# Four constants in one tile, and the two sides of SBUF moved by 32 and 96 bytes

## The chip, the cores and the metric

The kernel runs on one core of one Trainium2 chip. The metric is the time of one execution in device microseconds. Three runs of the kernel before gave 917.54, 922.28 and 922.48 us; their median is 922.28 us.

## The reference

Attention with pooled keys and values feeds a gated MLP, and this feeds a second MLP. With 4 batches, 8 heads, 576 positions and a head size of 64, in float32:

```python
k_p = k.reshape(B, H, 72, 8, D).mean(axis=3)          # pool 8 positions into one
v_p = v.reshape(B, H, 72, 8, D).mean(axis=3)
attn = softmax(q @ k_p^T / sqrt(D));  x = attn @ v_p   # -> x[2304, 512]
xn = x / sqrt(mean(x*x) + 1e-6) * rms_g
y = (silu(xn @ w_gate) * (xn @ w_val)) @ w_out         # 512 -> 1536 -> 512
h = y @ w_in2;  out = silu(h) @ w_out2                 # 512 -> 2048 -> 512
```

## The kernel before, in words

The 2304 tokens are eight chunks of 288 columns (`CH`). Activations stand transposed: features on the 128 partitions, tokens along the free dimension.

Nearly every product of the three MLP stages is made three times, so that float32 accuracy comes out of the faster matmul type `float32r`: each operand is split into a high and a low part of that type, and the kernel adds high by high, high by low and low by high. `mm3` (lines 256 to 259) and `mm3_open` (line 773) issue these triples. One tile of shape `[P, 2, n]` holds the high part first and the low part behind it, `4 n` bytes later in the same partition. For each matmul TensorE loads 128 columns of the stationary operand (a weight load, engine PEld) and streams the moving operand past it.

There are four large shapes of these float32r matmuls, by the number of moving columns:

- 288 columns, 9 groups of 240: the first MLP on chunks 0 to 4. Moving `xT` and `hT`, stationary `w_gate`, `w_val`, `w_out`.
- 432 columns, 9 groups of 96: the first MLP on chunks 5 to 7, taken as two halves of 432. Moving `xw` and `hw`, stationary the same weights.
- 384 columns, 1008: the way up of the second MLP (a Strassen-like scheme of 7 products), moving `xP1` to `xP7` (shown as `xP`), stationary `in`.
- 256 columns, 1512: its way down, moving `out2` (shown as `out`), stationary `hc`.

Besides these, chunks 2 to 7 of the attention make 3 products each for 4 head pairs with moving `pT` and stationary `vbd`, and one with moving `pR` (line 495); the scores (line 405) take `qT` as the stationary and `kbd` as the moving operand.

The order of all work is written out by hand in four long strings of steps (`start`, `pair`, `last`, `second`); nothing is rearranged by a scheduler. Every DMA is issued by the SP queue.

Where a tile lies decides the byte at which its rows begin. A tile pool takes the left side of SBUF, growing upwards, or the right side, growing downwards, and each tile's size is rounded up to 32 bytes. The pool `const` comes first on the left: `ident` with 512 bytes, then `ones`, `mhalf`, `g_sb` and `mask` with 32 bytes each, and later `scrap` with 32 bytes. On the left stand `stage`, `p1`, `att`, `pw` and `p2x`; on the right `w0`, `w1` (the weights of the first MLP, and the `early` tiles that share their places during the start) and `p2` (`h`, `s2`, `out2`).

In the program as built, the tiles that matter begin at these bytes past a multiple of 128:

| tiles | side | before |
|---|---|---|
| `xT`, `hT`, `xw`, `hw`, `xP`, `in`, `hc`, `kbd`, `vbd`, `vr`, `sq` | left | 32 |
| `w_gate`, `w_val`, `w_out`, `out2`, `h`, `early` tiles | right | 96 |
| `qT`, `pT`, `pR`, `kv`, `vs` (they lie behind three `kp` tiles of 288 bytes) | left | 0 |
| `ident` | left | 0 |

The low part lies 1152, 1536 or 1024 bytes behind the high part in the shapes of 288, 384 and 256 columns, which are multiples of 128, so both parts begin at the same remainder. In the shape of 432 columns it lies 1728 bytes behind, which adds 64 to the remainder.

Of the kernel before, what the change touches and what calls it, by code (L numbers as in the profile page):

```python
# [9 lines left out]
F32 = mybir.dt.float32  # L10
# [12 lines left out]
def tile_pooled_attention_then_two_mlps(  # L23
# [25 lines left out]
    P = 128  # L49
    KT = DM // P  # L50
# [5 lines left out]
    NTT = CH // TT  # L56
# [15 lines left out]
    EXP_SCALE = 1.0 / (POOL * math.sqrt(D))  # L72

    const = ctx.enter_context(tc.tile_pool(name="const", bufs=1))
    w_ctx = [ExitStack(), ExitStack()]
    w_pools = [x.enter_context(tc.tile_pool(name=f"w{i}", bufs=1, side="right")) for i, x in enumerate(w_ctx)]
    stage = ctx.enter_context(tc.tile_pool(name="stage", bufs=1))
# [13 lines left out]


    ident = const.tile([P, P], F32, name="ident")
    ones = const.tile([P, 1], F32, name="ones")
    mhalf = const.tile([P, NTT], F32, name="mhalf")
    g_sb = const.tile([P, KT], F32, name="g_sb")
    mask = const.tile([P, 4], F32, name="mask")

    def setup():
        make_identity(nc, ident)  # L100
# [1254 lines left out]
```

## Time and profile before

| | |
|---|---|
| runs | 917.54, 922.28, 922.48 us |
| the profiled execution, its own time | 922.12 us |
| its span, first to last instruction | 920.3 us |
| PE busy | 901.8 us, 98% of the span |
| weight loads (PEld) busy | 875.4 us, 95% |
| DVE, ACT, POOL busy | 631.2, 542.5, 375.8 us |
| mean granted clock of TensorE | 0.981 |

The profiled execution took 1.8 us more than its span, and 0.2 us less than the median. In the page's slices PE is at nine tenths or more in 38 of 40; the first slice has 5 and the last has 8. Matmuls overlap in the trace: one of 288 columns is shown with some 0.3 us, and the next one starts 0.13 us after it. So a shape's cost is read from the distance of starts, not from the mean length of one. How the matmuls' starts follow each other is read in the timeline; where many of one line follow each other it shows them as one row, with their count and their length from the first start to the last end.

### The profile page before, as it was taken

Reading aid. Unit: us, or ns where it says so; the run is one execution under the profiler, and the core shown is the slowest. Engines: PE = TensorE matmul, PEld = TensorE weight load, DVE = VectorE, ACT = ScalarE, POOL = GpSimd, SP = SyncE. Lnnn points to the kernel's source line nnn. Section 1 sums busy time; section 2 is a strip of 40 time slices with the busy share of each in tenths; the row PEclk is TensorE's granted clock in tenths of the full one; section 3 lists DMA queues with packets and bytes.
Section 4 is the critical chain, followed back from the end, with each engine's and each line's share of the span. In section 5 each row is a group of like instructions: output and inputs, shape, how many; then the busy total and the mean of one; then the engine's idle time right before and its main releaser. Section 6 shows DMA issues by size and latency. Waiting matters only on the chain.

```text
span 920.3 us, 17356 instructions
## 1 busy us (share of the span) xinstructions
PE 901.8 (98%) x6122; PEld 875.4 (95%) x6122; DVE 631.2 (69%) x1254; ACT 542.5 (59%) x1453; POOL 375.8 (41%) x487
## 2 busy tenths in 40 slices
PE   5999999999999999999999999999999999999998
PEld 4689999999999999999999998999999999999998
DVE  6789988765554835443368779658986579766675
ACT  5688887364254714345444546677666677576653
POOL 6435443344215621200027746881038910388200
PEclk8589999999999999999999999999999999999999
DMA  8645642342215321244367885266862668614486
GB/s 281 204 140 174 218 134 64 120 152 78 62 41 134 116 66 40 84 137 144 131 230 258 291 280 182 89 206 206 269 213 63 213 187 264 233 49 161 125 263 208
DMA packets 85259, 149.79 MB, mean 163 GB/s; under 512 B 8627, under 2 KB 53812, under 8 KB 85172
## 3 DMA queue, kind: packets, MB, share of 16 engines
q1 hardware_dynamic: 85172, 148.68, 50.0%
q8 instruction: 48, 0.79, 0.4%
q14 instruction: 39, 0.32, 0.1%
HBM read 116.21 MB, written 32.44 MB: 162 GB/s over the span
## 4 chain that ended last, share of the span: by engine, by line
PE 81%; DVE 9%; DMA 4%; POOL 3%; issue 2%; ACT 1%; SPq 0%; ACTq 0%; POOLq 0%; DVEq 0%
PE P L773 38%; PE pv L257 4%; PE pv L259 4%; PE pv L258 4%; PE pg L258 4%; PE pg L257 4%; PE pg L259 4%; PE acc L258 4%; PE acc L257 4%; PE acc L259 4%; PE sc L405 2%; PE pT L456 1%; PE pv L491 1%; DMA out<-out2s 1%; DMA xw_raw<-xw 1%
## 5 line engine op out<-in xcount | busy, mean ns | idle before, releaser
L773 PE MATMUL P<-xP,in 128*128 128x384 f32 x1008 | 179.5, 338 | 0.7 <-POOL in L244 0.5
L773 PEld LDWEIGHTS P<-xP,in 128*128 128x128 f32 x1008 | 177.5, 188 | 1.6 <-POOL in L244 0.8
L773 PE MATMUL P<-out,hc 128*128 128x256 f32 x1512 | 172.7, 276 | 0.0
L773 PEld LDWEIGHTS P<-out,hc 128*128 128x128 f32 x1512 | 172.5, 188 | 0.0
L244 POOL TENSOR_TENSOR in<-in,in 128x256 fp32r<-128x256 f32 x96 | 78.8, 830 | 112.1 <-ACT in L237 64.5
L237 ACT ACTIVATE hc<-h 128x384 fp32r<-128x384 f32 x144 | 74.1, 525 | 41.8 <-PE P L773 37.7
L244 DVE TENSOR_TENSOR hc<-h,hc 128x384 fp32r<-128x384 f32 x144 | 81.6, 590 | 19.6 <-ACT hc L237 17.7
L257 PE MATMUL pg<-xT,w_gate 128*128 128x288 f32 x240 | 73.0, 304 | 0.8 <-DVE hT L244 0.8
L257 PE MATMUL pv<-xT,w_val 128*128 128x288 f32 x240 | 73.0, 304 | 0.1
L257 PE MATMUL acc<-hT,w_out 128*128 128x288 f32 x240 | 72.4, 302 | 0.0
L258 PE MATMUL pg<-xT,w_gate 128*128 128x288 f32 x240 | 71.6, 298 | 0.2
L258 PE MATMUL acc<-hT,w_out 128*128 128x288 f32 x240 | 71.2, 297 | 0.2 <-DVE hT L244 0.2
L259 PE MATMUL pg<-xT,w_gate 128*128 128x288 f32 x240 | 71.2, 297 | 0.0
L259 PE MATMUL pv<-xT,w_val 128*128 128x288 f32 x240 | 70.9, 295 | 0.0
L258 PE MATMUL pv<-xT,w_val 128*128 128x288 f32 x240 | 70.8, 295 | 0.0
L259 PE MATMUL acc<-hT,w_out 128*128 128x288 f32 x240 | 70.8, 295 | 0.0
L423 ACT ACTIVATE pr<-sc,mx 96x72 f32<-96x72 f32 x192 | 57.9, 314 | 17.8 <-DVE mx L416 17.8
L624 ACT ACTIVATE th<-pg 128x288 f32<-128x288 f32 x57 | 23.5, 413 | 72.1 <-PE pg L259 71.9
L244 POOL TENSOR_TENSOR in<-sums,in 128x256 fp32r<-128x256 f32 x72 | 59.0, 829 | 2.4 <-ACT in L237 2.0
L626 DVE SCALAR_TENSOR_TENSOR th<-th,pg 128x288 f32<-128x288 f32 x57 | 25.6, 448 | 40.1 <-ACT th L624 40.0
L257 PEld LDWEIGHTS pg<-xT,w_gate 128*128 128x128 f32 x240 | 45.7, 190 | 1.3 <-issue 1.0
L258 PEld LDWEIGHTS pg<-xT,w_gate 128*128 128x128 f32 x240 | 45.6, 190 | 0.6 <-DVE xT L244 0.6
(233 smaller groups left out, 2304.4 us busy)
## 6 DMA issues: line engine op xcount, KB each, us to landing
out<-out SPq DMA_DIRECT2D x84, 512.0 KB, 4.7
out<-out2s SPq DMA_DIRECT2D x56, 256.0 KB, 4.1
in<-in SPq DMA_DIRECT2D x24, 512.0 KB, 3.6
raw<-in_moe_w_out_dram SPq DMA_DIRECT2D x18, 512.0 KB, 4.5
raw<-in_moe_w_in_dram SPq DMA_DIRECT2D x16, 512.0 KB, 3.7
early_raw<-in_moe_w_gate_dram SPq DMA_DIRECT2D x10, 512.0 KB, 4.2
early_raw<-in_moe_w_val_dram SPq DMA_DIRECT2D x10, 512.0 KB, 4.9
early_raw<-in_moe_w_out_dram SPq DMA_DIRECT2D x10, 512.0 KB, 4.8
```

Of the source, the lines that this page charges most:

```text
L237: nc.scalar.activation(out=out, in_=in_, func=AF.Copy, scale=1.0 if scale is None else scale)
L244: ENGINES[engine[0] or usual].tensor_tensor(out=out, in0=in0, in1=in1, op=op)
L257: nc.tensor.matmul(ps, lhsT=whi, rhs=xhi, start=first, stop=False)
L258: nc.tensor.matmul(ps, lhsT=whi, rhs=xlo, start=False, stop=False)
L259: nc.tensor.matmul(ps, lhsT=wlo, rhs=xhi, start=False, stop=last)
L405: nc.tensor.matmul(ps[:TT, a * 2 * SP:(a + 1) * 2 * SP], lhsT=qT[:, a * TT:(a + 1) * TT], rhs=kbd[:, j, :], start=True, stop=True,)
L423: nc.scalar.activation(out=pr[:, a, e], in_=s4[:, a, e], func=AF.Exp, bias=mx[:, a, e:e + 1], accum_out=sm[:, a, e],)
L456: nc.tensor.transpose(ps[:n, a * TT:(a + 1) * TT], src, ident[:TT, :TT])
L491: nc.tensor.matmul(ps, lhsT=vr0[:RR, j, :], rhs=pT_t[c, NPAIR + j // 2], start=False, stop=True)
L624: nc.scalar.activation(out=th, in_=pg, func=AF.Tanh, scale=0.5)
L626: nc.vector.scalar_tensor_tensor(out=th, in0=th, scalar=1.0, in1=pg, op0=ALU.add, op1=ALU.mult)
L773: nc.tensor.matmul(ps, lhsT=a, rhs=b, start=first and n == 0, stop=n == 2, skip_group_check=True)
```

## The change

Two unused tiles are added, and the four constants become slices of one tile `small`:

```diff
     const = ctx.enter_context(tc.tile_pool(name="const", bufs=1))
+    edge = ctx.enter_context(tc.tile_pool(name="edge", bufs=1, side="right"))
+    edge.tile([P, 24], F32, name="edge")
...
     ident = const.tile([P, P], F32, name="ident")
-    ones = const.tile([P, 1], F32, name="ones")
-    mhalf = const.tile([P, NTT], F32, name="mhalf")
-    g_sb = const.tile([P, KT], F32, name="g_sb")
-    mask = const.tile([P, 4], F32, name="mask")
+    small = const.tile([P, 16], F32, name="small")
+    ones, mhalf, g_sb, mask = (small[:, a:b] for a, b in ((0, 1), (1, 1 + NTT), (4, 4 + KT), (8, 12)))
+    const.tile([P, 8], F32, name="align")
```

`edge` takes 96 bytes at the right end, so every tile of the right side begins 96 bytes lower. On the left 64 bytes (`small`) and 32 (`align`) stand where 128 stood, so every tile behind them begins 32 bytes lower. The bytes past a multiple of 128 become:

| tiles | before | now |
|---|---|---|
| `xT`, `hT`, `xw`, `hw`, `xP`, `in`, `hc`, `kbd`, `vbd`, `vr`, `sq` | 32 | 0 |
| `w_gate`, `w_val`, `w_out`, `out2`, `h`, `early` tiles | 96 | 0 |
| `qT`, `pT`, `pR`, `kv`, `vs` | 0 | 96 |
| `ident` | 0 | 0 |
| low part of `xw`, `hw` | 96 | 64 |

A tile of the right side stood 64 bytes off one of the left, counted in remainders of 128, and now stands at the same remainder; two tiles of the same side keep their distance. No instruction is added, removed or moved: each engine has the same instructions in the same order with the same waits as before, and only the name `small` and the addresses differ.

## Rows read from the trace of the kernel before

**Rows 1.** Page: span, part 1, the chain that ended last by engine

```profile
span 920.3 us, 17356 instructions
PE 901.8 (98%) x6122; PEld 875.4 (95%) x6122; DVE 631.2 (69%) x1254; ACT 542.5 (59%) x1453; POOL 375.8 (41%) x487
...
PE 81%; DVE 9%; DMA 4%; POOL 3%; issue 2%; ACT 1%; SPq 0%; ACTq 0%; POOLq 0%; DVEq 0%
```

**Rows 2.** Groups by shape, PE: line, tiles, shapes, count, busy us, mean ns, idle

```profile
L773 PE MATMUL P<-xP,in 128*128 128x384 f32 x1008 | 179.5, 338 | 0.7 <-POOL in L244 0.5 <-ACT in L237 0.2
L773 PE MATMUL P<-out,hc 128*128 128x256 f32 x1512 | 172.7, 276 | 0.0
L257 PE MATMUL pv<-xT,w_val 128*128 128x288 f32 x240 | 73.0, 304 | 0.1
...
L257 PE MATMUL pg<-xw,w_gate 128*128 128x432 f32 x96 | 34.6, 360 | 0.0
...
L257 PE MATMUL pv<-pT,vbd 128*128 128x288 f32 x24 | 7.4, 310 | 0.0
```

**Rows 3.** Waits of PE: line, released by, us in total, times, longest

```profile
PE sc L405 <- POOL kbd L241: 8.9, 3, 7.3
```

**Rows 4.** Timeline of PE, 288 columns: start us, us, instruction

```profile
99.79 0.30 PE L258 MATMUL pv<-xT,w_val 128*128 128x288 f32 x1
...
104.30 0.29 PE L259 MATMUL pg<-xT,w_gate 128*128 128x288 f32 x1
```

**Rows 5.** Timeline of PE, 432 columns

```profile
499.77 0.36 PE L257 MATMUL pg<-xw,w_gate 128*128 128x432 f32 x1
...
502.71 0.36 PE L257 MATMUL acc<-hw,w_out 128*128 128x432 f32 x1
```

**Rows 6.** Timeline of PE, 384 and 256 columns, runs of matmuls in one row

```profile
599.78 3.51 PE L773 MATMUL P<-xP,in 128*128 128x384 f32 x19
...
911.73 4.81 PE L773 MATMUL P<-out,hc 128*128 128x256 f32 x41
```

**Rows 7.** Timeline of PE, products of the attention among those of an expert

```profile
209.33 0.30 PE L257 MATMUL pv<-pT,vbd 128*128 128x288 f32 x1
...
209.73 0.29 PE L495 MATMUL pv<-pR,vr 96*128 96x288 f32 x1
209.86 0.29 PE L257 MATMUL acc<-hT,w_out 128*128 128x288 f32 x1
...
211.44 0.30 PE L257 MATMUL pv<-pT,vbd 128*128 128x288 f32 x1
```

**Rows 8.** Groups by shape, weight loads (PEld) from 60 to 916 us

```profile
L405 PEld LDWEIGHTS sc<-kbd,qT 128*96 128x96 f32 x132 | 16.9, 163 | 0.2 <-ACT kbd L237 0.2
...
L528 PEld LDWEIGHTS ms<-ones,sq 128*96 128x96 f32 x36 | 3.7, 164 | 0.3
```

**Rows 9.** Groups by shape, DVE

```profile
L244 DVE TENSOR_TENSOR pT<-pT 128x288 fp32r<-128x288 f32 x24 | 10.9, 455 | 5.5 <-ACT pT L237 5.1
...
L244 DVE TENSOR_TENSOR hT<-pv,hT 128x288 fp32r<-128x288 f32 x21 | 9.4, 449 | 0.4 <-ACT hT L237 0.2
...
L342 DVE TENSOR_REDUCE kp<-kv 128x72 f32<-128x576 f32 x9 | 6.6, 739 | 0.0
...
L342 DVE TENSOR_REDUCE kp<-early 128x72 f32<-128x576 f32 x5 | 3.7, 733 | 3.5 <-DMA early<-in_k_dram 3.5
```

**Rows 10.** The chain in order of time, its first transfer: start us, us, what

```profile
1.22 4.26 DMA early<-in_k_dram
```

**Rows 11.** DMA issues: KB each, median us to landing

```profile
out_dram<-o SPq DMA_DIRECT2D x12, 128.0 KB, 3.5
```

**Rows 12.** Stretches: length, busy us of PE, PEld, DVE, ACT, POOL; granted clock

```profile
20.00:51.00 31.00, 30.46 (x106) 20.74 (x105) 22.29 (x48) 21.69 (x90) 16.01 (x23) 0.50 0.50 159
...
200.00:300.00 100.00, 100.00 (x776) 99.96 (x774) 55.34 (x129) 45.19 (x158) 39.30 (x60) 1.00 0.30 90
```

## The prediction

> **What bounds the kernel now.** I read the page first: PE is busy for 901.8 of 920.3 us, and the chain that ended last lies on PE for 81% of the span [rows 1]. Then PE's waits, to see whether that busy time is a queue without holes: the largest is 8.9 us in 3 waits at the scores of the start, one of them 7.3 us before the first matmul [rows 3]. The idle 920.3 - 901.8 = 18.5 us is thus this 8.9, the tail after the last matmul, and crumbs. Third the groups by shape, for the counts [rows 2]: 9 groups of 240 matmuls with 288 columns (2160), 9 of 96 with 432 (864), 1008 with 384, 1512 with 256. The mean length in these rows includes the overlap with the next matmul, so the price of one is read from the distance of starts in the timeline:
>
> - 288 columns: 35 matmuls begin from 99.79 to 104.30 us, both ends counted, so 4.51 / 34 = 132.6 ns [rows 4];
> - 432: 16 from 499.77 to 502.71, so 2.94 / 15 = 196.0 ns [rows 5];
> - 384: a run of 19 lasts 3.51 us, less the 0.338 us of the last [rows 2] over 18 steps: 176.2 ns [rows 6];
> - 256: a run of 41 lasts 4.81 us, less 0.276 over 40 steps: 113.4 ns [rows 6].
>
> Times the counts: 286.4 + 169.3 + 177.6 + 171.5 = 804.8 us, 87% of the span. So only two things can move the time much: the distance of starts of these 5544 matmuls, or new holes between them. The change adds and moves no instruction and no wait, so what is left is whether an instruction takes another time when its operands begin at other bytes.
>
> **The change part by part.**
>
> *Matmuls, the moving operand.* The trace has this experiment inside it: `pT` and `pR` begin at a multiple of 128 bytes, `hT` at 32 past one. At 209.33 us three products with moving `pT` and one with `pR` stand amid those of an expert, all of 288 columns: four steps from 209.33 to 209.86, 0.53 / 4 = 132.5 ns, and the twelve steps with moving `hT` after them, from 209.86 to 211.44, take 1.58 / 12 = 131.7 ns [rows 7]. The aligned operand is no faster; with starts rounded to 0.01 us, 0.8 ns is about what the rounding allows. So the moving operand's start byte costs nothing while the stationary operand begins at 32 or 96. I take 0.
>
> [...]
>
> *Matmuls, the stationary operand.* In the large shapes it begins at 32 or 96 in the whole trace; the nearest rows are weight loads of float32 with 96 columns at full clock: from `qT`, at 0, they take 163 ns, from `sq`, at 32, 164 ns [rows 8]. That is again no difference, but on loads that are not limited by a stream at full rate, so it is weaker evidence. I take 0 here too, because the row is near and the other ends below have no row that shows them.
>
> *Both ends for these two.* [...] A nearer end is the best rate that the kernel shows: 113.4 / 256 = 0.443 ns a column. At that rate the others take 127.6, 191.4 and 170.1 ns: 5.0 x 2160 + 4.6 x 864 + 6.1 x 1008 ns = 10.8 + 4.0 + 6.1 = 20.9 us less. From above: the worst rate is that of 288 columns, 0.460; with it the shapes of 256, 384 and 432 would take 117.8, 176.6 and 198.7: 4.4 x 1512 + 0.4 x 1008 + 2.7 x 864 ns = 6.7 + 0.4 + 2.3 = 9.4 us more.
>
> *Tiles that lose their start.* `qT`, `pT`, `pR`, `kv` and `vs` go from 0 to 96. By the same rows [7, 8] this costs nothing. If a misplaced start did cost a matmul 6 ns, the 72 products with `pT` (three groups of 24 [rows 2]) would give 0.4 us: too little to count.
>
> *The other engines.* They matter in the first 60 us, where PE waits for them, and wherever a buffer is late. The same instruction on tiles at both starts: DVE subtracts into `pT` (at 0) in 455 ns and into `hT` (at 32) in 449; it reduces `kv` (at 0) in 739 ns and an `early` tile (at 96) in 733 [rows 9]. A per cent, and against the aligned tile. I take 0; at 1% of the chain's DVE share of 9% [rows 1] it would be 0.8 us either way.
>
> *DMA.* Only the first load (4.26 us, into an `early` tile [rows 10]) and the last store (3.5 us [rows 11]) lie on the path with nothing beside them. Were they a tenth quicker or slower, it would be 0.8 us. The rest lands while PE works off its queue.
>
> *The small tile.* Two memsets, one reduction and one load write other bytes of it than before, and each reader reads its own slice. The waits are those of before, so no writer waits for another's slice: 0.
>
> Sum: 922.12 us of the profiled execution, of which 920.3 are its span, plus 0: 922.1 us, against a median of 922.28. I say 922.
>
> **The rivals.**
>
> *A, faster: the start byte does cost, but only goes away when both operands are aligned.* [...] Against it: the aligned `pT` should then have shown a part, and showed none [rows 7]. [...] Price: if all shapes came to the best rate, 20.9 us, so 901.
>
> [...]
>
> *B, slower: equal remainders collide.* The weight load reads SBUF while the stream does. In the shapes of 256 and 288 columns one operand lies left and the other right, 64 bytes apart in the remainder; now they are equal. [...] It would decide if 256 columns rose from 113.4 to about 117.8 ns: the 9.4 us from above, 931. Against it: per column 384 (0.459) is no worse than 288 (0.460), whose operands are 64 apart, and 432, where the low part has the remainder of the weights and the high part has not, has 0.454, between the others.
>
> *C, the change does not do what it says for the operands that count.* The low parts of `xw` and `hw` come to 64, and `pT` and `qT` lose their alignment. Their shares are 864 / 3 = 288 matmuls and the small ones above; whichever way starts matter, this turns A or B by some 2 us and is inside their prices.
>
> **How the numbers follow.** No change 0.50: the rows with both starts agree on three engines. A 0.30: the combination that it needs is in no row, and it touches 87% of the span. B 0.20: the rows are nearly as much against it, and it touches less. What this measurement can tell from no change is about 0.5%, 4.6 us: the runs before lie 4.9 us apart. A at 901 is beyond it, and so is B at 931, so these are the chances of faster and slower. The range goes from A's price, 901, to just short of B's, 930; below it lies the part of A that goes towards 868 or 855, above it the part of B that is worse than its price, together under 2 in 10. The forecast's own range is 917 to 926.
>
> **What would show it.** Right: starts of 288, 432, 384 and 256 columns 132.6, 196.0, 176.2 and 113.4 ns apart within 1 ns, waits of PE as before. [...] B: 256 columns rises while 384, whose operands keep their distance, stays at 176. The forecast would be wrong if any one of the four distances moved by more than 2 ns, or if PE waited anew while they stay.

## The result, and the profile after

The changed kernel takes 930.39 us (median of 6 runs, 927.34 to 931.68) against 922.25 us (6 runs beside them, 917.54 to 923.48): ratio 1.0091, 95% interval 1.0071 to 1.0112. It is slower, by 0.9%, and 0.4 us above the top of the range that was given.

The page of the changed kernel, with the lines that answer to [rows 1]:

```profile
span 929.9 us, 17356 instructions
PE 910.1 (98%) x6122; PEld 883.9 (95%) x6122; DVE 632.2 (68%) x1254; ACT 541.8 (58%) x1453; POOL 376.3 (40%) x487
...
PE 79%; DVE 10%; DMA 5%; POOL 3%; issue 2%; ACT 2%; SPq 0%; ACTq 0%; POOLq 0%; DVEq 0%
```

The count of instructions is the same, and DVE, ACT and POOL are busy as long as before within 1.0 us. PE has 8.3 us more of busy time in a span that is 9.6 us longer. Its groups by shape, against [rows 2] (line numbers are one higher; columns as there):

```profile
L774 PE MATMUL P<-out,hc 128*128 128x256 f32 x1512 | 180.7, 282 | 0.0
L774 PE MATMUL P<-xP,in 128*128 128x384 f32 x1008 | 179.4, 338 | 0.7 <-POOL in L245 0.4 <-ACT in L238 0.3
L258 PE MATMUL pv<-xT,w_val 128*128 128x288 f32 x240 | 73.2, 305 | 0.0
...
L258 PE MATMUL pg<-xw,w_gate 128*128 128x432 f32 x96 | 34.5, 359 | 0.0
...
L258 PE MATMUL pv<-pT,vbd 128*128 128x288 f32 x24 | 7.5, 314 | 0.0
```

One row moved: 256 columns, from 172.7 to 180.7 us. 384 columns (179.5 to 179.4) did not. PE's waits, against [rows 3], are the same within 0.4 us but for 0.9 us at the start, which is a wait of the attention's first scores:

```profile
PE sc L406 <- POOL kbd L242: 9.8, 3, 7.0
```

The cleanest view of the price is a place where nearly a third of the 256-column matmuls follow each other as one row of the timeline, and then a third of those of 384. Start, length, instruction, count; before:

```profile
744.74 55.30 PE L773 MATMUL P<-out,hc 128*128 128x256 f32 x486
799.88 58.37 PE L773 MATMUL P<-xP,in 128*128 128x384 f32 x330
```

and after:

```profile
749.02 57.94 PE L774 MATMUL P<-out,hc 128*128 128x256 f32 x486
806.79 58.34 PE L774 MATMUL P<-xP,in 128*128 128x384 f32 x330
```

The row of 486 less the mean length of its last matmul, over 485 steps: (55.30 - 0.276) / 485 = 113.45 ns before, as in [rows 6], and (57.94 - 0.282) / 485 = 118.88 ns after. The step of 384 columns is 176.4 and 176.3 ns. So 5.43 x 1512 = 8.2 us lie in this one shape. Over all steps between two following matmuls of a shape at the full clock (1.00 granted from 60 us on), 288 columns went from 132.54 to 133.08 ns and 432 from 195.4 to 196.2: 0.54 x 2160 + 0.8 x 864 = 1.9 us more. Together 10.1 us, where the span shows 9.6. The longer wait at the start is not felt behind it: after 200 matmuls, at 59.5 us, the changed kernel is only 0.1 us behind.

### The profile page after: what moved, and what is told of

It reads as the page before. It is cut to its first block, busy times and chain, and to the rows that moved or that the text cites. A ratio compares the mean times of both kernels' runs of the same rounds, so it can differ in the third digit from the quotient of the medians.

```text
span 929.9 us, 17356 instructions
## 1 busy us (share of the span) xinstructions
PE 910.1 (98%) x6122; PEld 883.9 (95%) x6122; DVE 632.2 (68%) x1254; ACT 541.8 (58%) x1453; POOL 376.3 (40%) x487
## 4 chain that ended last, share of the span: by engine, by line
PE 79%; DVE 10%; DMA 5%; POOL 3%; issue 2%; ACT 2%; SPq 0%; ACTq 0%; POOLq 0%; DVEq 0%
PE P L774 38%; PE pv L258 4%; PE pv L260 4%; PE pv L259 4%; PE pg L259 4%; PE pg L258 4%; PE pg L260 4%; PE acc L259 3%; PE acc L258 3%; PE acc L260 3%; PE sc L406 2%; DMA out<-out2s 1%; PE pT L457 1%; DMA raw<-in_moe_w_out_dram 1%; PE pv L492 1%
## 5 line engine op out<-in xcount | busy, mean ns | idle before, releaser
L774 PE MATMUL P<-out,hc 128*128 128x256 f32 x1512 | 180.7, 282 | 0.0
L774 PEld LDWEIGHTS P<-out,hc 128*128 128x128 f32 x1512 | 180.5, 190 | 0.0
L774 PE MATMUL P<-xP,in 128*128 128x384 f32 x1008 | 179.4, 338 | 0.7 <-POOL in L245 0.4
```

Source lines behind the costliest of these rows:

```text
L774: nc.tensor.matmul(ps, lhsT=a, rhs=b, start=first and n == 0, stop=n == 2, skip_group_check=True)
```

## The experiments

In what follows the *distance* is the first byte of the moving operand less that of the stationary operand, as a remainder of 128. The recorded expectations speak of these theories. **D**: the distance decides (rival B of the prediction, put more widely). **S**: a start at 0 itself is bad for the streams. **N** and **O**: a stream collides with the load of the next block, or with that of its own. **H**: address bits above 128 bytes count too. **T**: a table measured by itself holds in the kernel. **P**: what ran before counts. The other letters are explained in the expectation that uses them.

One table first; each run is told below it. The column "row" is the length of the timeline row of the 486 matmuls of 256 columns, with its step worked out as above.

| run | 256: distance, row, step | time, us | ratio to before [95%] |
|---|---|---|---|
| before | 64; 55.30; 113.5 ns | 922.25 | |
| after | 0; 57.94; 118.9 | 930.39 | 1.0091 [1.0071, 1.0112] |
| e1 | 96; 57.86; 118.7 | 930.62 | 1.0091 [1.0060, 1.0121] |
| e2 | 96; 57.85; 118.7 | 928.25 | 1.0070 [1.0046, 1.0093] |
| e3 | 64; 55.30; 113.5 | 920.78 | 0.9994 [0.9979, 1.0010] |
| e4 | 0; 57.94; 118.9 | 930.21 | 1.0093 [1.0072, 1.0113] |
| e5 | 64; 55.30; 113.5 | 921.49 | 1.0002 [0.9988, 1.0016] |
| e6 | 64; 55.30; 113.5 | 918.20 | 0.9972 [0.9954, 0.9990] |
| e7 | 64, places changed; 56.41; 115.7 | 925.06 | 1.0042 [1.0027, 1.0058] |
| e8 | high 64, low 0; 57.41; 117.8 | 926.86 | 1.0060 [1.0039, 1.0081] |
| e9 | 64; 55.26; 113.4 | 922.01 | 1.0011 [0.9994, 1.0028] |
| e10 | 64, places changed; 56.41; 115.7 | 923.00 | 1.0029 [1.0016, 1.0041] |
| e11 | 64, places changed; 57.40; 117.8 | 925.89 | 1.0051 [1.0033, 1.0070] |
| e12 | 48; 57.49; 118.0 | 927.54 | 1.0072 [1.0052, 1.0093] |
| e15 | 32; 57.05; 117.0 | 925.66 | 1.0047 [1.0031, 1.0062] |
| e16 | 32; 57.05; 117.0 | 926.04 | 1.0054 [1.0035, 1.0072] |
| e17 | 64; 55.30; 113.5 | 919.21 | 0.9981 [0.9968, 0.9995] |

**One side at a time (e1, e2).** e1 is the kernel before with the unused tile on the right alone, e2 the changed kernel without it:

```diff
 e1: +    edge.tile([P, 24], F32, name="edge")         # right 0, left stays 32
 e2: -    edge.tile([P, 24], F32, name="edge")         # left 0, right stays 96
```

> Only the right side moves, by 96 bytes: left tiles begin at 32, right tiles at 0 past a multiple of 128, so the two sides lie 32 or 96 apart. Theory D (what counts is the distance of the two operands' remainders; equal ones collide): 256 columns stay at 113 to 114 ns a matmul, as the products with pT, which lay 96 apart, cost no more than their neighbours; the time is that of before, 922 us. Theory S (a start at 0 is itself slow): the moving operand of 256 columns, out2, now starts at 0, and the weights of 288 and 432 do: if it is the stream's start, 256 columns rise to 119 ns and the time to 930 us; if it is the weight load's, 256 columns stay at 113 and 288 and 432 rise by about 1 ns, 925 us.

> Only the left side moves, by 32 bytes: left tiles at 0, right tiles at 96, 32 or 96 apart. Theory D: 256 columns stay at 113 to 114 ns, 922 us. Theory S: the stationary operand of 256 columns, hc, now starts at 0: if the weight load's start counts, 256 columns rise to 119 ns and the time to 929 us; if the stream's does, 256 stay, 288 rise by about 1 ns, 924 us.

Either half alone costs nearly the whole, 118.7 ns a step of 256 columns. D as these expectations put it, that only equal remainders are slow, is too narrow: a distance of 96 is slow as well. A start at 0 of the stream (S) is not needed: in e2 the stream stands at 96 as before, and is slow. But the stream begins at 0 in e1 and the weights do in e2, so a start at 0 of either one is not ruled out yet.

**Both ways of telling the start from the distance (e3, e4).** e3 brings both sides to multiples of 64 and keeps the distance at 64; e4 keeps the starts off any multiple of 64 and makes the distance 0:

```diff
 e3, from after:   -    edge.tile([P, 24], F32, name="edge")
                   +    edge.tile([P, 8], F32, name="edge")      # left 0, right 64
 e4, from before:  +    edge.tile([P, 16], F32, name="edge")     # left 32, right 32
```

> Left tiles at 0, right tiles at 64: both sides at multiples of 64, but 64 apart as in the kernel before. Theory D: all shapes as before (288: 132.5, 432: 195.5, 256: 113.5 ns), 922 us. Theory S: as the changed kernel or nearly so, 256 columns 118 to 119 ns, 930 us.

> Left and right tiles both at 32: no large operand is at a multiple of 64, but the remainders are equal, as in the changed kernel. Theory D: as the changed kernel, 256 columns 119 ns, 288 133, 930 us. Theory S: as before, 256 columns 113.5 ns, 922 us.

The same row of the timeline in e3, and then in e4:

```profile
741.83 55.30 PE L774 MATMUL P<-out,hc 128*128 128x256 f32 x486
```

```profile
748.79 57.94 PE L775 MATMUL P<-out,hc 128*128 128x256 f32 x486
```

e3 has the length of before and e4 that of after, to the hundredth of a microsecond over 485 steps, though e3 has the left side where the changed kernel has it and e4 has nothing at a multiple of 128. S falls: of the two, it is the distance that counts and not the start.

**The constants alone (e5).** The changed kernel without `edge`, its `align` tile of 64 bytes instead of 32, so that nothing behind `const` moves:

```diff
-    const.tile([P, 8], F32, name="align")
+    const.tile([P, 16], F32, name="align")
```

> The four constants in one tile, padded so that no other tile moves. Theory D (the time depends on the distance of the operands alone): as before, 256 columns 113.5 ns, 921 to 922 us. Rival: sharing the tile costs something by itself, at most what the start showed, 1 us.

1.0002 [0.9988, 1.0016]: the four constants in one tile cost nothing.

**The whole slowdown given back by one tile (e9, after e7).** In e7 `out2` alone, the stream of 256 columns, was put 64 bytes further inside a larger tile; that also changed how far its five buffers lie apart, from 4096 to 4224 bytes:

```diff
-        t = p2[0].tile([P, 2, 2, 256], F32R, tag="out2", bufs=5, name="out2")
+        t = p2[0].tile([P, 1056], F32R, tag="out2", bufs=5, name="out2")
+        t = t[:, 16:1040].rearrange("p (a e m) -> p a e m", a=2, e=2)
```

> The changed kernel, with out2 alone 64 bytes further, so that 256 columns have distance 64 again and all else is as in the changed kernel. Theory D: 256 columns 113.5 ns instead of 118.9, 8.0 us less: 922 us, with 288 columns still at 133.2 and 432 at 196.2. Rival G (the slowdown lies in more than the matmuls of this shape): above 925 us.

Only part came back, some 60%: 115.7 ns. e9 does it with 64 unused bytes ahead of the pool, the buffers 4096 apart as ever:

```diff
+            edge2.tile([P, 16], F32, name="edge2")    # pool on the right, opened just ahead of p2
             p2.append(ctx.enter_context(tc.tile_pool(name="p2", bufs=1, side="right", reuse_waits="tile")))
```

> The changed kernel with 64 unused bytes ahead of the right-hand pool of the second MLP, so that out2 lies 64 from hc again, its five buffers 4096 bytes apart as in the changed kernel (the earlier run that moved out2 alone had them 4224 apart). Theory D (distance in remainders of 128 is all): 256 columns 113.6 ns, 922 us; that the earlier run had 115.7 would then be due to something else. Theory H (address bits above 128 count as well, through the buffers' places): 256 columns 113.6 here too, since all five buffers stand at 832 past a multiple of 1024, a place that was fast there. Rival G (the slowdown is not in this shape alone): above 924 us.

e9 in the timeline:

```profile
743.48 55.26 PE L774 MATMUL P<-out,hc 128*128 128x256 f32 x486
798.57 58.34 PE L774 MATMUL P<-xP,in 128*128 128x384 f32 x330
```

113.4 ns and 922.01 us, 1.0011 [0.9994, 1.0028]. Everything else is as in the changed kernel, with 288 columns still at 133.1 and 432 at 196.1. So the shape of 256 columns carries what can be measured of the slowdown.

**The buffers' distance from each other, by itself (e10).** The kernel before with `out2` in the larger tile and no offset (`t[:, :1024]`):

> The kernel before with the five buffers of out2 4224 instead of 4096 bytes apart: every distance in remainders of 128 is as before (64), but the buffers stand at five places in 1024. Theory D: 256 columns 113.6 ns, 921 us. Theory H: 115 to 116 ns, 924 us, slow at some of the five places and 113.4 at others.

The distance of the operands is 64 and the step is 115.7 ns all the same, as in e7. A distance of 64 alone is thus not enough. Sorted by the half of a buffer that the stream comes from, five of the ten take 113.3 to 113.7 ns and the other five 117.5 to 118.3. So 115.7 is no third price but a mixture of two. The two halves of one buffer, 2048 bytes apart and so alike in every remainder up to 2048, lie one on each side.

**Which load (e8).** The low half of the late weights 64 bytes further (`[P, 2, HN + 16]` for `[P, 2, HN]` in `fr`), so that only the third product of a triple has a distance of 0 to its own block, and only the second to the next one:

> The kernel before, with the low half of the late tiles (weights in and hc) 64 bytes further behind the high half: in the shape of 256 columns the low weights lie 0 from the stream, the high ones 64 as before; in 384 columns the low ones 64, the high ones 0. In a triple (high by high, high by low, low by high) theory N (the stream of one matmul collides with the weight load of the next) has the second matmul of a triple of 256 columns take 119 to 120 ns and the others 113; theory O (a matmul is slowed by its own weights' place) has the third take it. Both: 256 columns on average 115.7 ns, 3 us more, 924 us, plus what 384 columns do.

All three products became slow (117.7, 118.1 and 117.6 ns from each to the next), which neither N nor O allows for.

**The other shapes (e6, e11, e12).** e6 puts 64 unused bytes ahead of the `xP` tiles of the kernel before, so that streams of 384 columns get a distance of 64 instead of 0; e11 adds 64 bytes between high and low part of `xw` and `hw`; e12 shifts `hc` and `in` by 16 bytes inside their tiles:

```diff
 e6:   +            p2x[0].tile([P, 16], F32, name="pad")
 e11:  -    pw[0].tile([P, 2, WB], F32R, tag="h", bufs=2, name="hw")      # xw alike
       +    pw[0].tile([P, 2, WB + 16], F32R, tag="h", bufs=2, name="hw")[:, :, :WB]
 e12:  -    pw[0].tile([P, 2, HN], F32R, ...)[:, :, :n]
       +    pw[0].tile([P, 2 * HN + 16], F32R, ...)[:, 4:4 + 2 * HN].rearrange("p (e m) -> p e m", e=2)[:, :, :n]
```

> The kernel before, with 64 bytes ahead of the pool that holds xP, so that the stream of 384 columns lies 64 from its weights instead of 0; the other shapes keep their distance. Theory D: as 256 columns gained 5.2 ns from 0 to 64, 384 columns fall from 176.3 to about 171 ns, 5 us less: 916 us. Rival F (the long shapes are limited by the stream's own rate, as 288 columns moved by less than 1 ns between all distances): 384 columns stay within 1 ns of 176.3, 921 us.

> The kernel before with xP 64 from its weights (918.2 us alone), and the low parts of xw and hw 1792 instead of 1728 bytes behind the high ones, so that both parts lie 64 from their weights. Theory D: the second matmul of a triple of 432 columns, which lay 0 from the weights and took 196 to 201 ns, falls to about 196, the shape's mean from 195.4 to 194: 1 us less, 917 us. Rival F: 432 columns stay at 195.4, 918 us.

> The kernel before with the late weights (hc, and nearly all of in) 16 bytes up: 256 columns have the distance 48 instead of 64, 384 columns 112 instead of 0. Theory D with a sharp place: 256 columns rise towards 118 to 119 ns as at 32 and 96, 928 us. With a broad place, half way between: about 116 ns, 924 us. 384 columns: between the 176.4 of distance 0 and the 174.4 of 64.

e6, and behind it e11 and e12, in the timeline:

```profile
739.86 55.30 PE L773 MATMUL P<-out,hc 128*128 128x256 f32 x486
795.00 57.70 PE L773 MATMUL P<-xP,in 128*128 128x384 f32 x330
```

```profile
745.20 57.40 PE L773 MATMUL P<-out,hc 128*128 128x256 f32 x486
802.44 57.80 PE L773 MATMUL P<-xP,in 128*128 128x384 f32 x330
```

```profile
747.15 57.49 PE L774 MATMUL P<-out,hc 128*128 128x256 f32 x486
804.48 57.92 PE L774 MATMUL P<-xP,in 128*128 128x384 f32 x330
```

In e6 384 columns fall from 176.4 to (57.70 - 0.337) / 329 = 174.4 ns: 2.0 x 1008 = 2.0 us, and the time falls with it, to 918.20 us. That lies between D, which had 171 ns, and F, which had less than 1 ns of change. This version beats the kernel before by 0.1% to 0.46%, and the changed one by more; it was run again inside e17 with 919.21. In e11 432 columns fall to 193.5 ns, as D had it, but the larger tiles put the `hc` that share their places 3584 instead of 3456 bytes apart, and 256 columns rise to 117.8: again at a distance of 64. In e12 16 bytes are enough to lose it (118.0).

Taken as a remainder of 256, the distance is 64 throughout the row of e11, since 3584 is 14 x 256; in the kernel before 3456 is 13.5 x 256, and it changes between 64 and 192 from one `hc` to the next. The kernel before, too, takes 117.7 ns on average in the first 12 steps of its row, nine at 64 and three at 192, and then 113.3 in all the others, at 64 as well as at 192. In e11, which never comes to 192, the step stays at 117.8. So the same distance goes with two prices inside the kernel, and neither a remainder of 128 nor one of 256 settles which.

**The effect by itself (e13, e14, e18).** These three kernels leave the reference's work out and run one block and one stream of one tile, 25 or 48 matmuls in a row, a matmul of 64 columns between rows:

```python
for n, points in ((256, 64), (288, 32), (432, 32), (384, 32)):      # e13
    for i in range(points):
        group(n, [(0, 512 + 4 * i)] * 25)       # (block, stream), in words of 4 bytes
```

> This kernel computes nothing of the reference: it writes zeros and runs rows of float32r matmuls of one stationary block and one stream in the same tile, 25 to a row, a matmul of 64 columns between rows. The stream begins 2048 bytes behind the block and then 16 bytes further in every row: 64 rows of 256 columns, 32 rows each of 288, 432 and 384. Theory D (the distance of the two addresses decides): the distance of starts in the 256-column rows repeats, about 118 to 119 ns where the distance is 0, 32, 48 or 96 past a multiple of 128 and 113.5 ns where it is 64, so 2 of 16 rows at least are fast and the period is 8 rows or a multiple of it. 288 columns: 132.3 to 133.2; 384: 176.4 at 0 and 174.4 at 64; 432: 193.4 at 64 and 196.2 at 0. Rival W (it is not the addresses but what else reads and writes SBUF in the kernel, or the split into three products): all rows of one shape alike within 0.5 ns. Rival S (the start alone): with the block at a fixed start it cannot be told from D here, but a period of 128 bytes or more in steps of 16 would then have to come from the stream alone, which e1 and e4 spoke against.

From e13, 256 columns: the rows at distances of 0, 96, 112, 160 and 192 past a multiple of 256 bytes, and 256 (the same as 0). Start, length, count:

```profile
30.91 3.23 PE L53 MATMUL acc<-a 128*128 128x256 f32 x25
...
49.33 3.24 PE L53 MATMUL acc<-a 128*128 128x256 f32 x25
...
52.44 3.14 PE L53 MATMUL acc<-a 128*128 128x256 f32 x25
...
61.60 3.24 PE L53 MATMUL acc<-a 128*128 128x256 f32 x25
...
67.80 3.10 PE L53 MATMUL acc<-a 128*128 128x256 f32 x25
...
79.97 3.24 PE L53 MATMUL acc<-a 128*128 128x256 f32 x25
```

The first step behind the small matmul is longer, some 200 ns. Without the first two steps of a row the mean is 119.5 to 120.0 ns in the slow rows shown and 115.5 and 114.2 in the rows of 3.14 and 3.10 us, and the 16 rows repeat every 256 bytes. These two means mix a start with what follows: both rows go on at 116 to 122 ns and end at steps of 113.3, the row at 192 from its sixth step on and that at 112 from its twelfth. Rival W falls: behind the first 32 us no other engine is busy here, and the DMAs move 1 GB/s. But a distance of 64 gave 117.7, not 113.5, and 192 gave 114.2: D's own number did not come back. The other shapes moved too: 288 columns between 130.0 and 133.7 ns, 384 between 173.1 and 178.5, 432 between 193.2 and 200.0.

> This kernel computes nothing of the reference: it writes zeros and runs rows of float32r matmuls of 256 columns. Rows 1 and 2: one block and one stream, distance 0 and 64 past a multiple of 128, 48 matmuls each. Rows 3 to 6: two blocks, L at remainder 0 and H at remainder 64, and two streams, at 0 and at 64, in patterns that give each stream a distance of 64 to its own block and 0 to the next (row 3), 0 to its own and 64 to the next (row 4), 0 to the next and 64 to the one before (row 5), 64 to the next and 0 to the one before (row 6). Theory N (a stream collides with the load of the next block, which runs beside it): row 1 slow (118 to 119 ns), row 2 fast (113.5), row 3 slow, row 4 fast, row 5 slow, row 6 fast. Theory O (with its own block): row 3 fast, row 4 slow, rows 5 and 6 in the middle. Theory V (with the one before): rows 3 and 4 slow and fast like N, row 5 fast, row 6 slow. Rows 7 to 14: block at 32 and at 64, stream 0, 32, 64 and 96 further: by theory D only the ones 64 further are fast, with both blocks. Then 64 rows with the distance 64 past a multiple of 128, each 128 bytes further, and 64 rows with 0. Theory H (bits above 128 count): among the first 64 rows some repeat slow ones, at about 117 to 118 ns, with a period of 512 to 4096 bytes, and the rest are at 113.5; without H all 64 are at 113.5 and the other 64 at 118 to 120.

The six pattern rows of e14, in the order of the expectation:

```profile
34.20 5.99 PE L53 MATMUL acc<-a 128*128 128x256 f32 x48
...
40.06 5.90 PE L53 MATMUL acc<-a 128*128 128x256 f32 x48
...
45.83 5.99 PE L53 MATMUL acc<-a 128*128 128x256 f32 x48
...
51.69 5.86 PE L53 MATMUL acc<-a 128*128 128x256 f32 x48
...
57.42 5.85 PE L53 MATMUL acc<-a 128*128 128x256 f32 x48
...
63.13 5.92 PE L53 MATMUL acc<-a 128*128 128x256 f32 x48
```

Row 3 (own 64, next 0) is as slow as row 1 (both 0), and row 4 (own 0, next 64) is quicker: that speaks against O. But row 5, which always has 0 to the next block, is the quickest, against N. V, the collision with the block before, has the order right: 117.0 and 116.8 ns in rows 4 and 5 against 119.8 and 118.1 in rows 3 and 6. But no row reaches V's 113.5, and in e8 V would have made one product of a triple slow, not all three. Of the 64 rows at a distance of 64 past a multiple of 128 every fourth was quick (113.6 ns) and the others, but for the very first, at 117.8, though their remainders of 256 only alternate between two values.

Rows 7 to 14 tell the start from the distance once more, without the kernel around. Shown are the distances of 32 and 64, first with the block at 32, then with the block at 64:

```profile
72.02 3.17 PE L53 MATMUL acc<-a 128*128 128x256 f32 x25
...
75.06 3.19 PE L53 MATMUL acc<-a 128*128 128x256 f32 x25
...
84.33 3.17 PE L53 MATMUL acc<-a 128*128 128x256 f32 x25
...
87.36 3.19 PE L53 MATMUL acc<-a 128*128 128x256 f32 x25
```

Moving block and stream together by 32 bytes changes next to nothing: at distances of 0, 32, 64 and 96 the steps are 120.0, 116.6, 117.9 and 120.0 ns with the block at 32, and 119.7, 116.6, 117.9 and 120.0 with the block at 64. But it is not 64 that is the quickest here, as D had it. So the distance counts, and yet does not give the price alone. e18 therefore ran the addresses of e13 in other orders:

```python
up = [4 * i for i in range(32)]
for order in (up, up[::-1], [16 + 32 * i for i in range(32)], [48] * 8):    # e18, 256 columns
    for d in order: group(256, [(0, 512 + d)] * 25)
```

> This kernel computes nothing of the reference: it writes zeros and runs rows of 25 float32r matmuls of 256 columns as e13, in the same tiles at the same addresses: 32 rows upwards in steps of 16 bytes, the same 32 rows downwards, 32 rows in steps of 128 bytes that begin at a distance of 64, and 8 rows at a distance of 192. Theory P (what ran before counts: stream and load lock into one of several rhythms): the distance of starts at one address differs between upwards and downwards by 2 ns or more in some rows, and of the rows in steps of 128 bytes, whose distance is 64 or 192, one in four is at 113.5 and the others at 117.8 as in e14, although e13 had 114.2 at 192 and 117.7 at 64. Theory A (the addresses alone): downwards mirrors upwards within 0.3 ns, the rows in steps of 128 bytes alternate between 117.7 and 114.2, and the last 8 rows are all at 114.2; then e14 differed because its tile lies at another place.

Two rows lie at a distance of 160 past a multiple of 256, going up (61.30 us) and down (192.91). The five others have the stream 2240 bytes behind the block (192 past a multiple of 256): going up (67.50), going down (186.87), in the steps of 128 bytes (229.63), and the first two of eight rows in which nothing but this distance is run (323.63, 326.69):

```profile
61.30 3.24 PE L53 MATMUL acc<-a 128*128 128x256 f32 x25
...
67.50 3.10 PE L53 MATMUL acc<-a 128*128 128x256 f32 x25
...
186.87 3.09 PE L53 MATMUL acc<-a 128*128 128x256 f32 x25
...
192.91 3.18 PE L53 MATMUL acc<-a 128*128 128x256 f32 x25
...
229.63 3.10 PE L53 MATMUL acc<-a 128*128 128x256 f32 x25
...
323.63 3.19 PE L53 MATMUL acc<-a 128*128 128x256 f32 x25
...
326.69 3.19 PE L53 MATMUL acc<-a 128*128 128x256 f32 x25
```

At 160 a step takes 120.0 ns upwards and 117.2 downwards. At 192 the same block and the same stream at the same addresses take 114.2, 113.4 and 113.6 ns in three places and 117.8 in the last eight rows. The end of the row going up, and a piece of the row at 326.69, show the two settled steps, 113.3 and 117.8 ns:

```profile
68.74 1.86 PE L53 MATMUL acc<-a 128*128 128x256 f32 x15
```

```profile
327.94 1.93 PE L53 MATMUL acc<-a 128*128 128x256 f32 x15
```

The rows take turns on two PSUM tiles, so that each distance has the other one going down than going up. That is not the reason: the rows at 229.63 and 326.69 write the same one and take 113.6 and 117.7 ns. The expectation's theory A (the addresses alone) falls, and the runs fit theory P: the same matmuls settle at one of several steps, and the order of the rows before them is what differs. How the rows before bring that about is not shown. A rule by addresses alone need thus not fit e7, e10 and e11.

**The table in the kernel (e15, e16, e17).** e15 and e16 were meant to place the weights of the first MLP 48 and 16 bytes from their streams, by unused tiles ahead of them on e6:

```diff
 e15: +    edge.tile([P, 28], F32, name="edge")      +    edge2.tile([P, 4], F32, name="edge2")
 e16: +    edge.tile([P, 20], F32, name="edge")      +    edge2.tile([P, 12], F32, name="edge2")
```

> e6 with 112 unused bytes ahead of the weights of the right side, so that streams of 288 columns lie 48 past a multiple of 128 from their blocks (64 in e6 and in the kernel before), and 16 more ahead of out2, which puts the streams of 256 columns back to 64. Theory T (the table of e13 holds in the kernel; high and low part of a stream lie 128 apart there, so that the mean of two rows of e13 counts): 288 columns at 48 and 176 past 256 took 130.2 and 131.6 ns, mean 130.9, against 131.5 and 133.4, mean 132.5, at 64 and 192, so 1.6 ns x 2160 = 3.5 us less; 432 columns about 1 ns more (0.9 us); 256 at 113.6 and 384 at 174.4 as in e6: about 915.6 us, ratio 0.9940 to the kernel before. Theory D alone (a distance of 64 is the good one, others cost): 288 columns rises to 133 and the time to 919.5 or more.

> As e15 with 80 unused bytes ahead of the weights and 48 ahead of out2: streams of 288 columns 16 past a multiple of 128 from their blocks, 256 columns at 64. Theory T: 288 columns at 16 and 144 took 131.7 and 129.95 ns in e13, mean 130.8: 1.7 ns x 2160 = 3.6 us less than e6; 432 columns between 195 and 197, as before or 1 ns more: about 915.5 us, ratio 0.9938. Theory D alone: 288 columns at 133.2, as it was at a distance of 0 and 32, so 919.5 us or more.

The edit missed its aim, since tiles are rounded up to 32 bytes: the weights came to a distance of 64 (e15, moved by 128) and 32 (e16), and `out2` to 32 in both. What they do tell: 256 columns at 32 is slow (117.0 ns), and 288 columns is 133.2 to 133.4 ns in both, in e15 at a distance of 64 as in the kernel before, which has 132.5. e17 moves `hT` by a slice inside its tile, which does reach 48:

```diff
-        hT[i, f] = t = p1.tile([P, 2, CH], F32R, tag="hT", bufs=2, name="hT")
+        hT[i, f] = t = p1.tile([P, 608], F32R, tag="hT", bufs=2, name="hT")[:, 28:604].rearrange("p (e n) -> p e n", e=2)
```

> e6 with hT, the stream of the third projection of the first MLP, 112 bytes into a tile that is 128 bytes longer: its high and low parts lie 48 and 176 past a multiple of 256 from their weights (64 and 192 in e6), those of xT stay. Theory T (the table of e13 holds in the kernel): products acc<-hT at 130.9 ns a matmul, pg<-xT and pv<-xT at 132.5 as before, 1.6 ns x 720 = 1.1 us less than e6, ratio 0.996 to the kernel before. Theory D alone: acc<-hT at 132.9 to 133.3. If the table does not carry over, because high and low part and two blocks alternate in the kernel, anything between 131.5 and 133.3, the time within 0.5 us of e6. 256 columns 113.6 and 384 columns 174 as in e6.

The products acc<-hT stay at 132.5 ns, where the table said 130.9, and the products with `xT`, which were not moved, are at 132.5 too. Theory T falls: the table of one block and one stream does not hold for the alternating products of the kernel. The time is that of e6 (919.21 us, 0.9981 [0.9968, 0.9995]).

## Why the prediction was wrong

- **What bounds the kernel** was right: PE's queue without holes, so that only the steps of the four shapes or new waits could move the time. The steps of [rows 4 to 6] moved, the waits did not.
- **"Matmuls, the moving operand ... I take 0" and "the stationary operand ... I take 0"** is where it failed: a term of 0 that turned out at 10.1 us, of which 8.2 lie in the 256 columns. Each operand was judged by itself, and what moved the step was the place of the two to each other. [Rows 7] compare `pT` at 0 with `hT` at 32, which is a distance of 96 beside one of 64, in the shape of 288 columns; that shape hardly answers (132.3 to 133.4 ns in all versions). [Rows 8] are loads beside streams of 144 columns (L405) and of one (L528), none of the four shapes. The shape that does answer, 256 columns, stood at a distance of 64 in the whole trace and had no row at another. So the steps of three shapes, 518 us or 56% of the span, were argued from rows of the fourth.
- **Rival B** was the outcome, and was given 0.20. Its price for 256 columns was 117.8 ns, measured 118.9; it expected 384 columns to stay, and they stayed; 432 rose by 0.8 where it had 2.7. Its sum of 9.4 us stands against 9.6 in the span, but that they are so near is in part luck: it had 6.7 us in 256 columns and 2.3 in 432, where 8.2 and 0.7 were measured, and nothing in 288, where it was 1.2. Its rule was too narrow: not only equal remainders are slow, distances of 32, 48 and 96 are as well (117.0 ns in e15, 118.0 in e12, 118.7 in e1), and so is 64 at times (117.8 in e11). The argument held against it, that 384 columns are no worse per column at a distance of 0, compared shapes with each other; e6 shows that 384 columns too were 2.0 ns worse than at 64.
- **The range** ended at 930, just short of B's own 931, on the ground that B is only a fifth. With so few rows against it, its price should have stood inside. The 868 and 855 that the range looks to below its lower end are terms that no run shows: the shortest mean steps of any run were 113.3, 130.0, 173.1 and 193.2 ns (256, 288, 384 and 432 columns; e13, e18), and the quickest kernel took 918.20 us (e6).
- **Rival A** (both aligned is faster) fell: no shape gained (256 columns 113.45 to 118.88 ns, 288 132.54 to 133.08, 432 195.4 to 196.2, and 384, aligned alike as well, 176.4 to 176.3). **Rival C** has nothing to turn, since the start is not what counts; the shape of 432 moved by 0.7 us.
- **The other engines, DMA and the small tile at 0** were right: DVE, ACT and POOL within 1.0 us, and e5 at 1.0002.
- **What would show it** named the right sign: 256 columns rise by more than 2 ns while 384 stay. It pointed to B: 256 columns rose by 5.4 ns and 384 stayed within 0.1.

All starts were multiples of 32 before and after the change, and the step of 256 columns was 113.4 ns before and 118.9 after. The place of the two operands to each other shows without the kernel around them too: in e13, with no other engine busy, moving the stream by 32 bytes, from a distance of 160 to one of 192 past a multiple of 256, changes the step from 120.0 to 114.2 ns, while in e14 moving block and stream together by 32 bytes changes it by no more than 0.3 ns.

What stays open is what collides. Shown is that the step changes with the address distance of stream and weights, and in this kernel by enough to make and unmake the whole slowdown (113.5 ns in e3, 118.9 in e4, 113.4 in e9). Shown too is that weight loads and matmuls run at the same time: 99.96 and 100.00 of 100 us busy [rows 12]. That the two meet in SBUF is a conclusion from this and was not seen; which load it would be (e8 and e14 fit none of N, O and V), and what makes the step settle at one price or the other, stay open.

## What to carry to other kernels

In this kernel, whose TensorE queue has no holes, an operand's place was a parameter of the matmul's price, by its distance to the other operand more than by its own alignment: for 256 columns it was worth 5% of their time (113.5 ns in e3, 118.9 in e4). Test a shape's price on rows of that very shape, and where the trace has none at another distance, keep the rival's price inside the range. After any change of tile sizes or pools compare the steps of long runs of matmuls in the timeline first; if one rose, a few unused bytes ahead of one pool may give it back (e9: 256 columns from 118.9 to 113.4 ns) or gain a little (e6: 384 columns from 176.4 to 174.4), and only a run tells which.

## What the runs showed of the hardware

- Steps of float32r matmuls at a granted clock of 1.00, by placement and by what ran before: 256 columns 113.3 to 120.0 ns, 288 130.0 to 133.7, 384 173.1 to 178.5, 432 193.2 to 200.0 (e13, e14, e18).
- The same matmul at the same addresses settles at a step of 113.3 or of 117.8 ns, and differs with the order of the rows before it (e18). The order given, it repeats: 57.94 us for 486 matmuls in after and in e4, whose distances are the same.
- A shift by 16 bytes matters (e12: 118.0 ns for 113.5), and so does how far buffers lie apart, 4224 instead of 4096 (e10: 115.7 ns) or 3584 instead of 3456 (e11: 117.8 ns), at one and the same distance in remainders of 128.
